# One dense batch instead of two in a block-sparse attention with a gated FFN: keys and queries of the block batches turned by TensorE, their V rows fetched through three queues

## The chip, the cores and the metric

The kernel runs on 1 core of one Trainium2 chip. The metric is the device time of one execution in microseconds (us); the median of three runs stands for a kernel. Everything said about the inside of an execution comes from one execution that the hardware profiler recorded.

## The reference

```python
# q, k, v: [4, 8, 768, 64] float32; sampled_blocks: [24, 3]; block = 32 positions, 24 blocks
scores = q @ k.transpose(0, 1, 3, 2) / sqrt(64)
mask = |blk_i - blk_j| <= 1  or  blk_i in (0, 23)  or  blk_j in (0, 23)
for qb in range(24):
    for kb in sampled_blocks[qb]:
        mask[block qb, block kb] = True
attn = softmax(where(mask, scores, -1e9)) @ v          # per batch and head
x  = attn, heads side by side: [3072, 512]
xn = x / sqrt(mean(x*x) + 1e-6) * rms_g
g  = xn @ w_gate                                       # [512, 1536]
out = (g * sigmoid(g) * (xn @ w_val)) @ w_out          # [3072, 512]
```

A query block so needs the first and the last key block, its neighbours, and three sampled ones, except for query blocks 0 and 23, which need all 24. The sampled block numbers are the same for all batches and heads, and they are known only when the kernel runs.

## The kernel before

A batch has 768 positions, that is six tiles of 128. The work is cut into units (`UNITS`, line 59): one to three tiles of one batch, for which attention, normalisation, FFN and output are done. The FFN of a tile is the largest part of TensorE's work: 96 projection matmuls per tile-equivalent (`proj`, L728, gate and value) and 12 output matmuls (`yy`, L767).

There are two kinds of batch, and `NDB` (line 51) says how many are of the first kind.

- A *dense* batch (0 and 1 before) computes all 768 keys for every query, and the mask is carried by 24 extra contraction rows (`AUG`, 64 + 24 = 88 rows). `dk` (L322) makes scores, `dexp` (L343) the exponentials, `dav` (L357) the product with V, `dxo` (L370) divides by the row sum. Keys and queries are turned so that the head dimension lies on partitions: batch 0 by TensorE (`tpx`, L301), batch 1 by DMA transposes from SP (`turn`, L288).
- A *block* batch (2 and 3 before) computes only the key blocks that are needed. Keys and queries are loaded, cast to bf16 (`fill_k`, `fill_q`), and turned by DMA transposes from SP (`turn_k` L478, `turn_q` L504). V is cast, written to a scratch tensor in HBM (`store_v`, L508), and read back as 32-row blocks by block number: `pair_v` (L570, L572, L578) fetches the blocks whose numbers are fixed, `block_v` (L555) the three sampled ones of a query block, whose row numbers sit in registers (`table_regs`, L435). The sampled key blocks are copied inside SBUF by GpSimd (`kg_sampled`), the fixed ones by VectorE or ScalarE (`kg_fixed`); both appear under the lines of the helper `copy` (ACT L144, POOL L146, DVE L148). `qk` (L599) and `exp` (L605) make an ordinary tile's scores and exponentials, `qka` (L615) and `expa` (L623) those of tile `AT`, which holds query blocks 0 and 23. `av` (L648) multiplies by V, `xo` (L659) divides.

After attention, for each unit: sum of squares (`sq`, L672 or L675), its inverse root (`rsq`, GpSimd L684, L686), scaling (`xq`, L693), a transpose to `xn` (by TensorE, `tr` L704, for the first `NPET` = 6 units, by a DMA transpose from SP, `xt` L715, for the later ones), then gate projection, tanh (`th`, ScalarE L737), `uu` (VectorE L743), value projection, `hp` (VectorE L754), output matmuls, `yo` (L777 or L779), and the store `so` (SP, L789 and L795).

The order of all this is made when the kernel is built. Every step is an operation with a list of engines that may do it, an estimated cost, steps that it depends on, and buffers that it takes and gives back. A loop (from L1204) always takes the operation that can start first by those estimates, with priorities deciding near-ties, and emits it. Each engine's instructions so stand in one fixed order, and an instruction that has to wait for a semaphore holds all that stands behind it on its engine. This holds for the queues that issue DMAs too: SP, ScalarE and GpSimd each issue theirs in order. The loads follow a list written out by hand (`seq`). Two of them are gated: `gate_sync` (L258) makes SP wait until a piece of the weights has landed. The weights themselves are loaded and cast by DMAs that GpSimd issues (L248, L252).

The pools that matter here: `vg` (gathered V tiles, 3), `kg` (gathered keys, 2), `xn`, `xq`, `xo` (2 units each), `hp` (2), `raw` (landing buffers for the block batches, 3).

Of the kernel before, what the change touches and what calls it, by code (L numbers as in the profile page):

```python
# [16 lines left out]
def kernel(  # L17
# [19 lines left out]
    P = 128  # L37
# [13 lines left out]
    NSLOT, NAUG, NOPEN, NDB = 5, 2, 2, 2  # L51
    IXAT, RGAT = 36.0, 48.0
    NPT, NPA, NKG, NVG, NRAW = 4, 2, 2, 3, 3
# [4 lines left out]
    HD = NC * D // 2  # L58
    UNITS = [(0, 0, 1), (0, 1, 1), (0, 2, 1), (0, 3, 3)]
    UNITS += [(b, c, 3) for b in range(1, NDB) for c in (0, 3)]  # L60
    ND = len(UNITS)
    for b in range(NDB, B):
        UNITS += [(b, (5, 0, 1), 3), (b, (2, 3, 4), 3)]
    NU = len(UNITS)
    HG = [("h", 0 if u < 3 else u) for u in range(NU)]
    HO = [u if u < 3 else 0 for u in range(NU)]
# [9 lines left out]
    def bank16(n):  # L76
# [12 lines left out]
    VAC = const.tile([P, 2, H * NC, D + 2], BF16, name="VAC")  # L89
    VGC = const.tile([P, 6, VW], BF16, name="VGC")  # L90
# [6 lines left out]
    RAWD = list(A)  # L97
    RAWS = [RAWC[:, i * RB:(i + 1) * RB] for i in range(NRAW)]
    aug = [AUG[:, i] for i in range(NAUG)]
    va_ = [VAC[:, i] for i in range(2)]  # L100
    vfl = [t.rearrange("p m d -> p (m d)")[:, 0:6 * VW] for t in va_]
    VAUG = [t.rearrange("p (t c h d) -> p t c h d", t=NC // 2, c=2, h=H) for t in (vfl[0], PTC[:, 10240:10240 + 6 * VW])]
    rt_ = RAWC[:, NRAW * RB:].bitcast(BF16)
    VGB = [VGC, rt_[:, 0:6 * VW].rearrange("p (x w) -> p x w", w=VW),
           vfl[1].rearrange("p (x w) -> p x w", w=VW)]
    PD = [PTC[:, i * PDW:(i + 1) * PDW] for i in range(3)]
    PTB = [t.rearrange("p (h l x) -> p h l x", h=2, l=2) for t in [rt_[:, 6 * VW:6 * VW + 1024]] + [
        PTC[:, i * 1024:(i + 1) * 1024] for i in range(NPT - 1)]]
    PAB = [PTC[:, 3072 + i * 2048:3072 + (i + 1) * 2048].rearrange("p (l h x) -> p l h x", l=2, h=2) for i in range(NPA)]
    KTB = [t.rearrange("p (a s) -> p a s", a=NP) for t in (xs_[3], xs_[1])]  # L110
    QTB = [t.rearrange("p (a s) -> p a s", a=NP) for t in (xs_[4], PTC[:, 7168:7168 + NP * S])]
    KGB = [xs_[i].rearrange("p (x a s j c) -> p x a s j c", x=6, a=NP, s=4, j=16) for i in (0, 2)]
    KROW = AUG[:, 0].rearrange("p i e c x -> p (i e c x)").rearrange(
        "p (a c t x) -> p a c t x", a=NP, c=2, t=NC // 2)
    QROW = AUG[:, 1].rearrange("p i e c x -> p (i e c x)").rearrange("p (a n x) -> p a n x", a=NP, n=NC)
    kvv = [t.rearrange("b h (t p c) d -> b p (h t) (c d)", p=P, c=2) for t in (k, v)]
    qvv = q.rearrange("b h (n p) d -> b n p h d", p=P)
# [32 lines left out]
    zt = const.tile([P, VW], BF16, name="zt")  # L150
# [36 lines left out]
    nc.gpsimd.memset(zt[0:32, P:VW], 0.0)  # L187
# [9 lines left out]
    for t in va_:  # L197
        nc.vector.memset(t[:, :, D:D + 1], 1.0)
# [72 lines left out]
    def load(g, i):  # L271
        b, pr = divmod(g, NP)
        if i == 0:
            rawd[g] = RAWD[held["rawd", g][1]]
        nc.sync.dma_start(out=rawd[g][:, i], in_=(kv, qv, vv)[i][b, :, 2 * pr:2 * pr + 2, :])

    def fill(g, i, eng):
        copy(eng, aug[g % NAUG][:, i, :, :, 0:D],
             rawd[g][:, i].rearrange("p h (c d) -> p h c d", d=D))

    def pad_v(g, eng):
        b, pr = divmod(g, NP)
        src = rawd.pop(g) if b else A[g]
        copy(eng, va_[b][:, 2 * pr * NC:2 * (pr + 1) * NC, 0:D],
             src[:, 2].rearrange("p h (c d) -> p (h c) d", d=D))

    def turn(g):
        nc.sync.dma_start_transpose(  # L288
            out=X[g % NSLOT].rearrange("p i e (c t) -> p (i e c) t", t=P),
            in_=aug[g % NAUG].rearrange("p i e c r -> p (i e c r)"))  # L290

    def zero_pad(i):
        nc.vector.memset(aug[i][:, :, :, :, KQ:P], 0.0)
# [15 lines left out]
    held, rawd = {}, {}  # L309
# [38 lines left out]
    def dav(u, pr, bk):  # L348
        b, c0, nt = UNITS[u]
        pt, va = pts.pop((u, pr)), va_[b]  # L350
        o_ = PS[:, bk[0], 0:nt * 2 * (D + 1)].rearrange(
            "p (t e d) -> p t e d", t=nt, e=2)
        tiles["o", u, pr] = o_
        for t in range(nt):
            for e in range(2):
                for jt in range(NC):
                    nc.tensor.matmul(  # L357
                        out=o_[:, t, e, :], lhsT=pt[:, jt, e, t * P:(t + 1) * P],
                        rhs=va[:, (2 * pr + e) * NC + jt, 0:D + 1],
                        start=(jt == 0), stop=(jt == NC - 1))  # L360
# [14 lines left out]
    tab_, at_ = VGB[0].rearrange("p x w -> p (x w)"), [0]  # L375

    def small(n, dt, p=P):
# [7 lines left out]
    kti, vti = small(NS * 2, I32, 1), small(NS * NR, I32, 1)  # L385
    koff, voff = {}, {}

    REGS = {"POOL": [("k", 0, 16), ("k", 16, 32), ("k", 32, 2 * NS)], "SP": [("v", 0, 16), ("v", 16, 32), ("v", 32, 2 * NS)],
            "ACT": [("v", 2 * NS, 2 * NS + 11), ("v", 2 * NS + 11, 3 * NS)]}
    HALF = 1024  # L390

    def load_table():
        nc.sync.dma_start(
            out=stab.rearrange("p n r i -> p (n r i)"), in_=s64.rearrange("n x -> (n x)").unsqueeze(0))
        for b in range(NDB, B):
            for lo in (0, S + 32):
                nc.sync.dma_start(out=vrows[b][lo:lo + 32, :], in_=zt[0:32, :])

    def table(i, eng):
# [3 lines left out]
        elif i == 1:  # L403
            TC(out=sf, in_=stab[:, 1:NB - 1, :, 0])
            TS(out=d2, in0=sf, scalar1=16.0, scalar2=None, op0=ALU.mult)
            TC(out=kti[:, 0:NS], in_=d2[:, :, 0])
# [16 lines left out]
        else:  # L423
# [4 lines left out]
            TS(out=vti.rearrange("p (r n) -> p n r", r=NR), in0=d2, scalar1=32.0, scalar2=32.0, op0=ALU.mult, op1=ALU.add)  # L428
# [3 lines left out]
    def table_regs(eng, part):  # L432
        e = {"POOL": nc.gpsimd, "ACT": nc.scalar, "SP": nc.sync}[eng]
        w, lo, hi = REGS[eng][part]
        _, got_ = nc.values_load_multi_w_load_instructions(  # L435
            {"k": kti, "v": vti}[w][0:1, lo:hi], engines=[e.engine], min_val=0,
            max_val={"k": 16 * (NB - 1) * (HALF + 1), "v": 32 * (NB + 1)}[w], skip_runtime_bounds_check_because=WHY)
        for i_, x in enumerate(got_):
            r, n = divmod(lo + i_, NS)
            {"k": koff, "v": voff}[w][n * NR + r] = x  # L440

    def k_at(n, r):
        x = koff[n * NR + min(r, 1)]
        if r:
            x = x >> 10 if r == 2 else x & (HALF - 1)
        return nc.s_assert_within(x, 0, 16 * (NB - 1), skip_runtime_bounds_check_because=WHY)


    def load_kv(b, i, hf):
        key = ("kv"[i], b, hf)  # L450
        raws[key] = RAWS[held["raw", key][1]]
        nc.sync.dma_start(
            out=raws[key].rearrange("p (x y) -> p x y", y=2 * D),
            in_=kvv[i][b, :, 3 * HH * hf:3 * HH * (hf + 1), :])

    def load_q(b, n):
        key = ("q", b, n // 3)
        raws[key] = RAWS[held["raw", key][1]]
        nc.sync.dma_start(
            out=raws[key][:, n % 3 * DM:(n % 3 + 1) * DM].rearrange("p (h d) -> p h d", h=H), in_=qvv[b, n])  # L460

    def fill_k(b, hf, c, eng):
        src = raws["k", b, hf].rearrange("p (a e t c d) -> p a e t c d", a=NP // 2, e=2, t=NC // 2, c=2)
        dst = KROW[:, NP // 2 * hf:NP // 2 * (hf + 1)].rearrange("p a c t (e d) -> p a c t e d", e=2)
        copy(eng, dst[:, :, c].rearrange("p a t e d -> p a e t d"), src[:, :, :, :, c, :])

    def fill_v(b, hf, c, eng):
        src = raws["v", b, hf].rearrange("p (h t c d) -> p h t c d", h=HH, t=NC // 2, c=2)
        vaugs[b] = VAUG[held["va", b][1]]
        copy(eng, vaugs[b][:, :, c, HH * hf:HH * (hf + 1), 0:D].rearrange("p t h d -> p h t d"), src[:, :, :, c, :])  # L470

    def fill_q(b, i, eng):
        copy(eng, QROW[:, :, 3 * i:3 * i + 3, :].rearrange("p a n x -> p n a x"),
             raws["q", b, i].rearrange("p (n a x) -> p n a x", n=3, a=NP))

    def turn_k(b):
        KTs[b] = KTB[held["KT", b][1]]
        nc.sync.dma_start_transpose(  # L478
            out=KTs[b].rearrange("p a (n x) -> p (a n) x", x=P), in_=KROW.rearrange("p a c t x -> p (a c t x)"))

    def tpk(b, pr, bk):
        t_ = bank16(bk[0])[:, 0:S].rearrange("p (c t x) -> p c t x", c=2, x=P)
        tiles["tk", b, pr] = t_
        for c in range(2):
            for t in range(NC // 2):
                nc.tensor.transpose(out=t_[:, c, t, :], in_=KROW[:, pr, c, t, :], identity=ident)

    def evk(b, pr, eng):
        KTs[b] = KTB[held["KT", b][1]]
        copy(eng, KTs[b][:, pr, :], tiles.pop(("tk", b, pr)).rearrange("p c t x -> p (c t x)"))  # L490

    def tpq(b, n, bk):
        t_ = bank16(bk[0])[:, 0:NP * P].rearrange("p (a x) -> p a x", x=P)
        tiles["tq", b, n] = t_
        for pr in range(NP):
            nc.tensor.transpose(out=t_[:, pr, :], in_=QROW[:, pr, n, :], identity=ident)

    def evq(b, n, eng):
        QTs[b] = QTB[held["QT", b][1]]
        copy(eng, QTs[b][:, :, n * P:(n + 1) * P], tiles.pop(("tq", b, n)))  # L500

# [821 lines left out]
```

## Time and profile before

| what | value |
|---|---|
| median of 3 runs | 305.85 us (304.5 to 306.33) |
| profiled execution | 307.95 us; its span 306.2 us |
| TensorE matmuls | 284.4 us busy, 93% of the span, 3838 instructions |
| VectorE | 195.1 us, 64% |
| ScalarE | 175.2 us, 57% |
| GpSimd | 80.3 us, 26% |
| DMA | 48.50 MB moved, mean 158 GB/s; 48037 of 85204 packets under 512 B |
| granted TensorE clock, mean | 0.989 of full |

The span is the time from the first to the last instruction of the program in the profile; the profiled execution's own time is 1.75 us longer. Matmuls are pipelined: a busy time counts each matmul from its start to its end, so a mean of 300 ns for one does not mean that one starts every 300 ns. What one costs in a stream is read from runs in the chain of work that ended last, where a piece has a length and a count. In the list of waits, a row says which instruction sat idle before it started and what released it.

### The profile page before, as it was taken

Reading aid. Unit: us, or ns where it says so; the run is one execution under the profiler, and the core shown is the slowest. Engines: PE = TensorE matmul, PEld = TensorE weight load, DVE = VectorE, ACT = ScalarE, POOL = GpSimd, SP = SyncE. Lnnn points to the kernel's source line nnn. Section 1 sums busy time; section 2 is a strip of 40 time slices with the busy share of each in tenths; the row PEclk is TensorE's granted clock in tenths of the full one; section 3 lists DMA queues with packets and bytes.
Section 4 is the critical chain, followed back from the end, with each engine's and each line's share of the span. In section 5 each row is a group of like instructions: output and inputs, shape, how many; then the busy total and the mean of one; then the engine's idle time right before and its main releaser. Section 6 shows DMA issues by size and latency. Waiting matters only on the chain.

```text
span 306.2 us, 9818 instructions
## 1 busy us (share of the span) xinstructions
PE 284.4 (93%) x3838; PEld 183.4 (60%) x3838; DVE 195.1 (64%) x462; ACT 175.2 (57%) x290; POOL 80.3 (26%) x196
## 2 busy tenths in 40 slices
PE   8999989889999998999779699998699999999995
PEld 7899877666666664665445345564255655546543
DVE  6688896576756755877568435767177958807700
ACT  4899874468888785368554226877065424413322
POOL 4648100010024615119754200755041000100000
PEclk9999999999999999999999979999989999999999
DMA  7999999864799996783987973333754400060032
GB/s 218 364 242 157 203 268 323 182 229 80 119 267 266 182 308 161 159 239 87 263 196 187 195 157 97 90 84 89 166 127 135 92 36 2 0 156 0 1 98 109
DMA packets 85204, 48.50 MB, mean 158 GB/s; under 512 B 48037, under 2 KB 81318, under 8 KB 85158
## 3 DMA queue, kind: packets, MB, share of 16 engines
q1 hardware_dynamic: 76946, 41.63, 54.7%
q0 software_dynamic: 5792, 4.72, 10.1%
q10 hardware_dynamic: 2420, 1.53, 2.0%
q8 instruction: 30, 0.49, 0.6%
q14 instruction: 16, 0.13, 0.1%
HBM read 36.70 MB, written 8.02 MB: 146 GB/s over the span
## 4 chain that ended last, share of the span: by engine, by line
PE 67%; DMA 14%; DVE 8%; issue 5%; SPq 2%; ACT 2%; ACTq 1%; DVEq 0%
PE PS L728 33%; PE PS L767 15%; PE PS L322 7%; PE PS L357 4%; DMA RAWC<-in_v_dram 4%; PE PS L648 3%; DMA XC<-AUG 2%; DMA RAWC<-in_k_dram 2%; PE PS L301 2%; DMA VGC<-vrows 2%; DVE uu L743 2%; PE PS L599 2%; DMA xn<-xq 1%; DVE hp L754 1%; ACT th L737 1%
## 5 line engine op out<-in xcount | busy, mean ns | idle before, releaser
L737 ACT ACTIVATE th<-PS 128x384 bf16<-128x384 f32 x96 | 46.5, 492 | 81.9 <-PE PS L728 37.5
L743 DVE SCALAR_TENSOR_TENSOR uu<-th,PS 128x384 bf16<-128x384 bf16 x96 | 52.4, 551 | 49.4 <-ACT th L737 47.1
L728 PE MATMUL PS<-xn,wg 128*128 128x384 bf16 (+1 forms) x480 | 74.3, 294 | 7.3 <-DVE uu L743 4.2
L343 ACT ACTIVATE PTC<-PS 128x768 bf16<-128x768 f32 x92 | 70.4, 815 | 14.0 <-PE PS L322 13.8
L728 PE MATMUL PS<-xn,wv 128*128 128x384 bf16 (+1 forms) x480 | 77.9, 297 | 0.1
L767 PE MATMUL PS<-wo,hp 128*128 128x512 bf16 (+1 forms) x300 | 71.4, 376 | 4.1 <-DVE uu L743 4.1
L754 DVE TENSOR_TENSOR hp<-uu,PS 128x384 bf16<-128x384 bf16 x96 | 52.0, 551 | 16.8 <-PE PS L728 14.7
L728 PEld LDWEIGHTS <-wg 128*128 128x128 bf16 x480 | 40.7, 98 | 31.4 <-issue 9.0
L146 POOL COPY XC<-XC 128x128 bf16 x132 | 39.3, 371 | 62.6 <-PE PS L599 35.7
L728 PEld LDWEIGHTS <-wv 128*128 128x128 bf16 x480 | 40.5, 98 | 23.9 <-issue 1.9
L767 PEld LDWEIGHTS <-hp 128*128 128x128 bf16 x300 | 29.0, 99 | 32.4 <-issue 6.2
L322 PE MATMUL PS<-XC 88*128 88x128 bf16 (+1 forms) x288 | 42.6, 276 | 0.6 <-ACT PTC L343 0.6
L322 PEld LDWEIGHTS <-XC 88*128 88x128 bf16 x288 | 22.2, 100 | 7.8 <-issue 0.9
L357 PE MATMUL PS<-VAC,PTC 128*128 128x65 bf16 x552 | 21.1, 193 | 0.2 <-DVE XO L370 0.2
L357 PEld LDWEIGHTS <-PTC 128*128 128x128 bf16 x552 | 20.0, 97 | 2.0 <-issue 0.3
L777 ACT ACTIVATE yo<-PS 128x512 f32<-128x512 f32 (+1 forms) x16 | 9.1, 571 | 20.2 <-PE PS L767 20.1
L146 POOL CAST AUG<-RAWC 128x768 bf16<-128x768 f32 (+3 forms) x12 | 11.6, 973 | 30.1 <-DMA RAWC<-in_k_dram 25.7
L693 DVE SCALAR_TENSOR_TENSOR xq<-XO,rs,gB 128x512 bf16<-128x512 f32 x24 | 18.5, 792 | 0.2 <-POOL rs L686 0.2
L686 POOL TENSOR_TENSOR rs<-ms,nhalf 128x1 f32<-128x1 f32 (+1 forms) x6 | 4.3, 714 | 47.8 <-DVE ms L675 47.8
L605 ACT ACTIVATE PTC<-PS 128x1024 bf16<-128x1024 f32 x15 | 15.2, 1022 | 1.6 <-PE PS L599 1.1
L648 PEld LDWEIGHTS <-PTC 128*32 128x32 bf16 x736 | 8.1, 97 | 8.7 <-issue 7.4
L599 PEld LDWEIGHTS <-XC 64*128 64x128 bf16 x480 | 7.5, 93 | 6.9 <-issue 5.8
(112 smaller groups left out, 225.1 us busy)
## 6 DMA issues: line engine op xcount, KB each, us to landing
out_dram<-yo SPq DMA_DIRECT2D x21, 256.0 KB, 2.0
RAWC<-in_k_dram SPq DMA_DIRECT2D x4, 768.0 KB, 5.7
RAWC<-in_v_dram SPq DMA_DIRECT2D x4, 768.0 KB, 10.6
RAWC<-in_q_dram SPq DMA_DIRECT2D x12, 256.0 KB, 5.3
RAWC<-in_v_dram SPq DMA_DIRECT2D x7, 384.0 KB, 6.5
RAWC<-in_k_dram SPq DMA_DIRECT2D x6, 384.0 KB, 6.6
wg<-in_moe_w_gate_dram POOLq DMA_DIRECT2D x4, 384.0 KB, 6.9
wv<-in_moe_w_val_dram POOLq DMA_DIRECT2D x4, 384.0 KB, 7.9
```

The costliest lines, as they stand in the source:

```text
L146: nc.gpsimd.tensor_copy(out=out, in_=in_)
L322: nc.tensor.matmul(out=s_[:, e, j * w:(j + 1) * w], lhsT=x[0:KQ, 0, e, jt * P:(jt + 1) * P], rhs=x[0:KQ, 1, e, c0 * P:c0 * P + w], start=T ...
L343: nc.scalar.activation(out=pts[u, pr][:, g * kt:(g + 1) * kt].rearrange("p j e w -> p e j w"), in_=s_[:, :, 0:kt * w].rearrange("p e (j w) ...
L357: nc.tensor.matmul(out=o_[:, t, e, :], lhsT=pt[:, jt, e, t * P:(t + 1) * P], rhs=va[:, (2 * pr + e) * NC + jt, 0:D + 1], start=(jt == 0), ...
L605: nc.scalar.activation(out=t_.rearrange("p h l x -> p (h l x)"), in_=tiles.pop(("s", b, n, pp)).rearrange("p h l x -> p (h l x)"), func=AF ...
L648: nc.tensor.matmul(out=o_[32 * i:32 * i + 32, a, :], lhsT=l_, rhs=r_, start=i not in begun, stop=k_ == last[i], tile_position=(0, 32 * i), ...
L693: nc.vector.scalar_tensor_tensor(out=xqs[u][:, t, :], in0=xos[u, t].rearrange("p h d -> p (h d)"), scalar=mss[u][:, t:t + 1], in1=gB, op0= ...
L728: nc.tensor.matmul(out=p_[:, j, :].rearrange("p (t w) -> p t w", w=P), lhsT=w_[:, c, f_ * P:(f_ + 1) * P], rhs=xns[u][:, :, c, :], start=( ...
L737: nc.scalar.activation(out=t_, in_=tiles["gp", u, f], func=AF.Tanh, scale=0.5)
L743: nc.vector.scalar_tensor_tensor(out=t_, in0=tiles.pop(("th", u, f)), scalar=1.0, in1=tiles.pop(("gp", u, f)), op0=ALU.add, op1=ALU.mult)
L754: nc.vector.tensor_tensor(out=hps[u][:, f * fg:(f + 1) * fg, :], in0=tiles.pop(("uu", u, f)), in1=tiles.pop(("vp", u, f)), op=ALU.mult)
L767: nc.tensor.matmul(out=tiles["yp", u, t, h], lhsT=hps[u][:, f, t * P:(t + 1) * P], rhs=wo[:, f, x], start=(f == 0), stop=(f == NF - 1))
```

## The change

- Batches 1, 2 and 3 are block batches now, batch 0 alone is dense (`NDB` = 1). Dense batch 1 disappears with its loads, its four DMA transposes and its V layout.
- A block batch's units are smaller: batch 1 has units of 1, 2, 1 and 2 tiles, batch 2 of 1, 2 and 3, batch 3 of 3 and 3. There are 13 units instead of 10; the first six are still those whose `xn` is turned by TensorE.
- Keys, queries and values of a block batch are loaded in two halves of four heads each, partition p taking positions 6p to 6p+5, which makes a contiguous run of 6 x 64 float32, 1536 bytes. Before, the runs were of 512 bytes (k, v) and 256 bytes (q).
- They are turned by 12 TensorE transposes per half (`turn`), copied from PSUM by ScalarE (`turned`) into position order. The scratch rows of V follow the same order (`store_v`).
- In tile `AT`, the first score matmuls take every sixth column of the turned keys as weights.
- The sampled V blocks of a query block (r = 0, 1, 2) are issued by SP, ScalarE and GpSimd; before, by SP (r = 0, 1) and ScalarE (r = 2). Two row numbers share a register, so ScalarE and SP load one set of 11 each; GpSimd's row number rides in its key register.
- Buffers: `vg` 4 instead of 3, `pt` 5 (shared by the `AT` tiles). A wait for the first value halves on a piece of the weights stands where it stood for dense batch 1.

The core of the diff, in the order of the file:

```diff
-    NSLOT, NAUG, NOPEN, NDB = 5, 2, 2, 2
+    NSLOT, NAUG, NOPEN, NDB = 5, 2, 2, 1
-    NPT, NPA, NKG, NVG, NRAW = 4, 2, 2, 3, 3
+    NPT, NKG, NVG, NRAW = 5, 2, 4, 3
+    SPLIT = (((5,), (0,1), (2,),( 3, 4)), ((5,), (0, 1), (2, 3, 4)), ((5, 0, 1), (2, 3, 4)))
     UNITS = [(0, 0, 1), (0, 1, 1), (0, 2, 1), (0, 3, 3)]
-    UNITS += [(b, c, 3) for b in range(1, NDB) for c in (0, 3)]
...
-        UNITS += [(b, (5, 0, 1), 3), (b, (2, 3, 4), 3)]
+        UNITS += [(b, ns, len(ns)) for ns in SPLIT[b - NDB]]
...
-    kvv = [t.rearrange("b h (t p c) d -> b p (h t) (c d)", p=P, c=2) for t in (k, v)]
-    qvv = q.rearrange("b h (n p) d -> b n p h d", p=P)
+    kvv = [kv, vv, qv]
...
+    REGS = {"POOL": [("k", 0, 16), ("k", 16, 32), ("k", 32, 2 * NS)],
+            "DVE": [...], "ACT": [("v", 0, NS // 2)],
+            "SP": [("w", 0, NS // 2)]}
...
+            TT(out=kti[:, 0:NS], in0=d1[:, :, 2], in1=k0f, op=ALU.add)
+            for t_, r in ((vti, 1), (wti, 0)):
+                TT(out=t_, in0=d1[:, NS // 2:NS, r], in1=d2[:, 0:NS // 2, r], op=ALU.add)
...
+            out=raws[key].rearrange("p (h y) -> p h y", h=HH), in_=kvv[i][b, :, HH * hf:HH * (hf + 1), :])
...
-    def turn_k(b):
-        nc.sync.dma_start_transpose(...)
...
+    def turn(b, x, j, bk):
+        t_ = PS[:, bk[0]:bk[0] + 2].rearrange("p b x -> p b x").bitcast(BF16)[:, :, 0:S].rearrange(
+            "p a (c w) -> p a c w", w=P)
+        tiles["turn", b, x, j] = t_
+        for a in range(2):
+            for c in range(NC):
+                nc.tensor.transpose(out=t_[:, a, c, :], in_=(KROW if x == "k" else QROW)[:, 2 * j + a, c, :], identity=ident)
+
+    def turned(b, x, j, eng):
+        ts, tb, n_ = (KTs, KTB, "KT") if x == "k" else (QTs, QTB, "QT")
+        ts[b] = tb[held[n_, b][1]]
+        copy(eng, ts[b][:, 2 * j:2 * j + 2, :].rearrange("p a (w c) -> p a c w", c=NC), tiles.pop(("turn", b, x, j)))
...
     def store_v(b):
         nc.sync.dma_start(
-            out=vrows[b][32:S + 32, :].rearrange("(t p c) f -> p t (c f)", p=P, c=2),
+            out=vrows[b][32:S + 32, :].rearrange("(p t) f -> p (t f)", t=NC),
...
-            copy(eng, kg[:, x, :, :, r, :], kt[:, :, :, bass.ds(kb, 16)])
+            copy(eng, kg[:, x, :, r, :], KTs[b][:, :, bass.ds(k_at(blocks(n)[x] - 1, r, eng), 32)])
...
-        (nc.scalar if r == 2 else nc.sync).dma_start(
+        (nc.sync, nc.scalar, nc.gpsimd)[r].dma_start(
...
-                    lhsT=KTs[b][HS[h], pr, m * P:(m + 1) * P] if m < NC else ...
+                    lhsT=KTs[b][HS[h], pr, m::NC] if m < NC else ...
...
+    CE = {1: (DP_, DP_, DP_), 2: (P_,D_,D_), 3: (DP_,DP_,P_)}      # engines of the casts of v, k, q
+    TTE, TTP = ("ACT",), -1
+    KDE, CPE = ("POOL", ), ("DVE", "ACT")
...
+        for x in "kq":
+            for j in range(2):
+                op(("tt" + x, b, j), {"PE": 12 * 0.056}, [("sf" + x, b, j, c) for c in range(2)], (TTP, b, j),
+                   lambda e, p, a=(b, x, j): turn(*a, p), [(S_, ("tt" + x, b, j))], [(x + "row", b)])
+                op(("turn" + x, b, j), pick_({"ACT": 1.45, "DVE": 1.75}, TTE), [("tt" + x, b, j)], (-0.5, b, j),
+                   lambda e, p, a=(b, x, j): turned(*a, e), [(x.upper() + "T", b)], [(None, ("tt" + x, b, j))])
...
+                for x in xs[::2]:
+                    op(("gv",) + G + (x,), {"SP": 2 * GVC}, sts + rgs["SP", "w"], (GVP, order, x),
+                       lambda e, p, a=G, x=x: [block_v(*a, x_, 0) for x_ in (x, x + 1)], [("vg", T)], d=0.2)
+                for x in xs:
+                    for r, e_, c_, w_ in ((1, "ACT", GVC, "v"), (2, "POOL", GPC, "k")):
+                        op(("gw",) + G + (x, r), {e_: c_}, sts + rgs[e_, w_], (GWP, order, x),
+                           lambda e, p, a=G + (x, r): block_v(*a), [("vg", T)])
```

## The prediction

> **What bounds the kernel now.** I read the page's slices first, then busy time by stage, the list of waits and the chain that ended last.
>
> ```profile
> PE   8999989889999998999779699998699999999995
> PEclk9999999999999999999999979999989999999999
> DMA  7999999864799996783987973333754400060032
> ```
>
> TensorE is 90% busy or more in most slices. It falls off in the sparse stage (slices 20 to 29), where PEclk dips twice.
>
> ```profile
> 62.00:120.00 58.00, 57.09 (x588) 37.50 (x587) 39.26 (x82) 46.31 (x69) 13.87 (x22) 1.00 0.94 207
> 120.00:250.00 130.00, 116.33 (x1962) 66.26 (x1961) 82.40 (x182) 67.09 (x118) 46.57 (x135) 0.97 0.58 142
> ```
>
> Columns: stretch, its length, busy us of PE, PEld, DVE, ACT, POOL, granted clock, DMA share, GB/s. Dense batch 1 (62 to 120) leaves PE 0.9 us idle. The two block batches (120 to 250) leave 13.7 us, and the clock costs 3.3 more: ten-us stretches show 0.84 at 170 and 0.83 at 220. That is 17.0 us that PE does not stream, 8.5 per block batch.
>
> ```profile
> PE PS L728 <- DVE uu L743: 4.2, 6, 1.2
> PE PS L767 <- DVE uu L743: 4.1, 2, 3.0
> PE PS L728 <- DMA xn<-xq: 3.1, 1, 3.1
> ACT th L737 <- DMA VAC<-vrows: 13.4, 2, 10.6
> ACT th L737 <- DMA VGC<-vrows: 6.0, 2, 3.5
> ACT th L737 <- DMA XC<-AUG: 5.8, 1, 5.8
> ```
>
> Columns: total us, times, longest. PE waits for `uu`, which waits for ScalarE's tanh, which stands in ScalarE's queue behind work that waits for a DMA. Two places in the chain (start, length, what) name those DMAs:
>
> ```profile
> 167.34 6.75 DMA XC<-AUG
> 175.04 0.50 ACT th L737
> ...
> 215.88 4.16 DMA xn<-xq
> ```
>
> So it is a PE-bound kernel with a leak in the block batches.
>
> **The change, part by part.** The profiled execution took 307.95 us, span 306.2; the median is 305.85. I work out a difference against the 306.2 and apply it to the median. Spacings of PE come from runs in the chain:
>
> ```profile
> 32.13 0.67 PE PS L728 x12
> ...
> 70.03 0.75 PE PS L704 x12
> ...
> 71.43 1.14 PE PS L357 x36
> 72.57 0.65 PE PS L322 x4
> ...
> 154.17 0.68 PE PS L599 x44
> ...
> 195.54 0.61 PE PS L615 x36
> ...
> 205.88 0.83 PE PS L648 x64
> ```
>
> *PE stream.* Dense batch 1 goes: 96 score matmuls at 0.1625 (0.65/4) are 15.6 us, 288 of P·V at 0.0317 are 9.1: -24.7. Its block form comes: 240 at 0.0155, 72 at 0.017, 448 at 0.013: +10.7. Turning K and Q on PE: 144 transposes at 0.0625 (the L704 row, the same kind of instruction): +9.0. Transposes of xn fall from 48 to 36: -0.75. Narrower units: a one-tile unit's projections cost 96 x 0.0558 = 5.36 us a tile against 96 x 0.1625/3 = 5.20. Three more such units are +0.5; six tiles in two-tile units have no row, lie between 0 and +1.0, and I take 0.5. Sum: **-4.8**. The 144 score matmuls whose weights are now read with a step of six elements have no row either: 0 if the load stays under the matmul, at most +5.9 by the slowest weight load (L301, 138 ns mean against 97); I take 0, since weight loads of 93 to 100 ns sit under matmuls 16 ns apart in L599.
>
> The Trainium skill (TensorE: Matmul & The Clock Gate, Part 4: PE-mode transpose) speaks against this: about 275 ns per transpose in one kernel, and the full clock does not engage for transposes. Here L704 takes 219 ns each, but twelve pass in 0.75 us at clock 1.00. By the page's figure as a spacing, the 144 would be 39.6 us and the kernel slower; the trace decides.
>
> *The K and Q transposes by DMA go.* There were eight, which held SP's queue for 3.6 to 6.4 us each. The one at 167.34 shows on PE as 3.03 us idle (busy 6.97 of 170 to 180) plus 1.6 of clock: **-4.6**. The other end is 0, if the PSUM copy on ScalarE that takes its place comes as late.
>
> *V rows from three queues.* SP issues 22 single blocks per block batch instead of 44, beside some 17 pair and edge pieces: 39 in place of 61, a third less. From 140 to 160 PE is 4.2 us short (9.03 and 6.74 busy), waiting for gathered rows and for work behind them. I take half: **-2.1** (0 to -4.2). At 211 to 215.9 SP was issuing V rows while the finished `xq` (last DVE piece ends 210.7) waited for its transpose behind them; 210 to 220 is short 4.06 us, plus 1.7 of clock. Half again: **-2.9** (0 to -5.8). Against it: seven units, not four, now take that DMA transpose.
>
> *What it adds on ScalarE, VectorE, GpSimd and DMA*, costed at nothing under PE's FFN work. ScalarE loses 48 exponentials (39 us at 0.815) and gains 14 of 1.02, 12 PSUM copies of 1.44 (the 128x1536 copy to xn took 1.44), some 20 copies of 0.48 and 22 issues of 0.32: about +9 on 175, less 7 for output copies that pass to VectorE. If the cover goes, the tanh is late next, then `uu`, then PE. VectorE gains about 9 on 195 (12 normalisations at 0.60 and 12 output copies at 0.68, minus 8 normalisations at 0.75). DMA moves some 5 MB more of V rows in a stretch at share 0.58. The loads in 1536-byte runs get no credit: the dense batches' 384 KB in such runs landed in 6.5 us, 768 KB in short runs in 5.7 and 10.6.
>
> GpSimd needs its own budget, per block batch:
>
> ```profile
> L146 POOL COPY XC<-XC 128x128 bf16 x132 | 39.3, 371 | 62.6 <-PE PS L599 35.7 <-PE PS L322 10.5 <-DMA XC<-AUG 8.3
> L248 POOL DMA_DIRECT2D wg<-in_moe_w_gate_dram x4 | 3.5, 887 | 0.0
> L248 POOL DMA_DIRECT2D wv<-in_moe_w_val_dram x4 | 3.1, 786 | 0.0
> ```
>
> 66 sampled copies at 0.371 are 24.5; 22 new issues at 0.85 (the weight loads, the only issues from this queue; the lower end is ScalarE's 0.32, the upper the first one's 1.15) are 18.7; casts 5, rsqrt 4: 52 us. PE needs about 61 for the same batch (six tiles at 5.2 + 2.6 of FFN, 10.7 attention, 3 transposes). It fits, with 9 us to spare.
>
> The Trainium skill (SBUF — State Buffer, SBUF: two separate sides) speaks against GpSimd as issuer: while VectorE runs a copy in a two-port mode GpSimd cannot write descriptors, and 620 ns became 3100. The eight weight issues above took 0.74 to 1.15 us in stretches with VectorE 80% busy. By the page's 3.1 the 22 issues are 68 us and GpSimd bounds the kernel, some 40 us per batch slower; by the row, nothing.
>
> *Register loads.* ScalarE loads its row numbers once instead of twice (4.1 and 5.4 us at 50 and 57). PE is 1.7 us short from 50 to 70: **-0.9**.
>
> *A third block batch.* Of the 17.0 us, 17.0 - 4.6 - 2.1 - 2.9 = 7.4 stay for two batches, so the third brings **+3.7** (1.2 if only what I could not place recurs, 8.5 if nothing is mended).
>
> *Hand-over from dense to block.* Before, batch 1 was dense and covered all preparation of batch 2. Now batch 1 is fetched behind the weights (gates at 32.3 and 36.3, unchanged). V's second half, issued 36.9, lands by 47.5 (10.6); casts behind register loads (3.6 each on GpSimd) end near 53; the store, K's second half and Q follow on SP's queue and land near 65; six V issues on GpSimd (5.1) stand before Q's cast; transpose and PSUM copy (0.75 + 1.44) make the first score possible near 73. PE had its last dense P·V at 59.6 and in the new order some 25 groups of 0.67 before that score: near 75. The margin of 2 is smaller than the spread of one landing (5.7 to 10.6). I take one wait as long as the two of 3.0 and 3.1 seen: **+3.0** (0 to 5).
>
> Sum: -4.8 - 4.6 - 2.1 - 2.9 + 3.7 - 0.9 + 3.0 = -8.6, so 305.85 - 8.6 = **297.3 us**, the span near 297.6.
>
> **Rivals.**
> *ScalarE's queue decides (slower).* 66 V-row issues stand in it in place of 44, each waiting for a buffer or for the store, with tanh behind them. Then block batches cost what they cost now, 17.0/44 = 0.39 us per issue, so 22 more are +8.5; the ScalarE copy stands in the same queue, so the 4.6 is not saved; nothing is halved: -4.8 + 8.5 - 0.9 + 3.0 = +5.8, 311.7 us. It decides once such a wait exceeds the two groups (1.3 us) that PE has in hand. For it: the 21 us of tanh waiting for V rows. Against: a fourth V buffer.
> *Block batches run without leaks (faster).* All bounds at their good end: -4.8 - 4.6 - 4.2 - 5.8 + 1.2 - 1.7 + 0 = -19.9, 286 us. For it: units of one and two tiles give PE other units' FFN in each chain; SP's queue loses 33 us of transposes. Against: ScalarE, VectorE and GpSimd would all be near 80% there, in fixed order.
> *GpSimd bounds.* From 1.25 us per issue it passes PE's 61; at 2.0 that is 16.5 per batch, 347 us. Against: the highest row is 1.15.
> *The PE saving alone, leaks as large as before plus a third batch's 3.7 and the hand-over:* about 307, no change.
>
> **How the numbers follow.** Main case 0.40, leak-free 0.20, ScalarE 0.24, GpSimd 0.04, no change 0.12. A measurement of this kernel tells about 1% (3 us) from no change. Faster by over 1%: nearly all of the main case and the leak-free one, 0.58; within 1%: 0.14; slower: 0.28. The main case's own range is 291 to 303; leaving out two in ten, 287 to 313.
>
> **What would show it.** Right: transposes on PE 12 in about 0.75 us; no PE wait behind a K transpose; PE short by about 11 us over the three block batches; GpSimd's V issues near 0.85 us and GpSimd under PE; a wait of about 3 us between 60 and 76. Wrong: tanh waiting over 30 us in all for V rows (ScalarE's case), GpSimd issues over 1.25 us, or block-batch idle as large per batch as now.

## The result, and the profile after

The changed kernel takes **337.22 us** (median of 4 runs, 334.84 to 341.73); the kernel before took 305.96 beside it. The ratio is 1.1006, 95% interval 1.0902 to 1.111: 10% slower, where 297.3 us was forecast. The profiled execution took 335.35 us; its span is 333.8. A run more than 1.5% above the fastest of its kernel is left out of every ratio, so a ratio need not be that of the two medians.

The page's slices of the changed kernel (rows: TensorE, ScalarE, granted clock):

```profile
PE   8997899587779967969578869999999999999995
ACT  5998376178986899795967599557717422422310
PEclk9999599878979997879879999999999999999999
```

TensorE has holes from 58 to 200 us (a slice is 8.3 us), the clock falls in or just behind the same places (and at 33 to 42, behind a smaller hole), and ScalarE is at 8 or 9 in most of them. Busy time by stage, first of the changed kernel, then of the kernel before (columns: stretch, its length, busy us of PE, PEld, DVE, ACT, POOL, then clock, DMA share, GB/s):

```profile
20.00:80.00 60.00, 50.41 (x701) 41.84 (x703) 36.89 (x108) 37.83 (x47) 17.14 (x26) 0.89 0.84 190
80.00:230.00 150.00, 124.34 (x2475) 89.65 (x2490) 80.61 (x179) 120.19 (x135) 83.14 (x231) 0.92 0.55 157
```

```profile
20.00:80.00 60.00, 56.97 (x836) 45.05 (x834) 44.83 (x126) 44.41 (x69) 8.27 (x13) 1.00 0.95 202
80.00:230.00 150.00, 136.55 (x2099) 80.67 (x2095) 93.44 (x203) 89.82 (x148) 58.46 (x153) 0.98 0.75 172
```

Length less busy time times clock is what TensorE does not stream. Before it is 3.0 us in the first stretch and 16.2 in the second; after, 60 - 50.41 x 0.89 = 15.1 and 150 - 124.34 x 0.92 = 35.6. That is 31.5 us more, while the span grew by 27.6: by this difference TensorE's own work shrank by some 4 us, and waits ate it several times over. The clock is part of the loss: of the 35.6 us, 25.7 are idle time and 9.9 are lost to the lower clock.

In the list of waits (us in total, times, longest), V rows in front of tanh are a small item now (in the changed kernel L702 is tanh, L708 `uu`, L468 the new transposes, L580 the first scores of tile `AT`, L148 a ScalarE copy):

```profile
DVE uu L708 <- ACT th L702: 65.6, 42, 8.3
PE PS L580 <- ACT XC L148: 5.4, 2, 3.1
PE PS L468 <- ACT XC L148: 4.8, 2, 2.7
ACT th L702 <- DMA VXC<-vrows: 4.5, 1, 4.5
```

Tanh waited 19.4 us for V rows in the two largest rows before; now 4.5 and 3.2. Yet `uu` waits for tanh 65.6 us, up from 47.1, and TensorE waits for ScalarE's copies. The groups of instructions, shapes apart (count | busy us, mean ns | idle before), show why:

```profile
L148 ACT COPY XC<-PS 128x1536 bf16<-128x1536 bf16 x8 | 42.3, 5292 | 9.1 <-PE PS L468 9.1
L148 ACT COPY VXC<-PS 128x1536 bf16<-128x1536 bf16 x4 | 21.2, 5298 | 5.3 <-PE PS L468 5.3
```

The twelve copies of turned keys and queries (`turned`, through `copy`) take 5.29 us each. The forecast had 1.44. Together they are 63.5 us instead of 17.3. ScalarE's timeline shows what such a copy does:

```profile
139.37 5.31 ACT L148 COPY XC<-PS 128x1536 bf16<-128x1536 bf16 x1 [0.68 <-PE PS L468]
144.29 0.81 ACT L702 ACTIVATE th<-PS 128x512 bf16<-128x512 f32 x1
144.99 5.29 ACT L148 COPY XC<-PS 128x1536 bf16<-128x1536 bf16 x1
```

```profile
145.87 1.28 PE L693 MATMUL PS<-xn,wg 128*128 128x256 bf16 x8 [2.83 <-DVE uu L708]
```

One tanh comes through between two copies. TensorE (second fence, its timeline) stands for 2.83 us until `uu` behind that tanh frees its bank.

### The profile page after: what moved, and what is told of

It reads as the page before. It is cut to its first block, busy times and chain, and to the rows that moved or that the text cites. A ratio compares the mean times of both kernels' runs of the same rounds, so it can differ in the third digit from the quotient of the medians.

```text
span 333.8 us, 11910 instructions
## 1 busy us (share of the span) xinstructions
PE 292.1 (88%) x4605; PEld 206.4 (62%) x4634; DVE 198.3 (59%) x470; ACT 210.3 (63%) x269; POOL 131.5 (39%) x343
## 4 chain that ended last, share of the span: by engine, by line
PE 62%; ACT 13%; issue 9%; DMA 7%; DVE 3%; ACTq 2%; SPq 1%; POOLq 1%; POOL 1%; DVEq 0%
PE PS L693 33%; PE PS L732 14%; ACT XC L148 7%; PE PS L613 4%; DMA wg<-in_moe_w_gate_dram 4%; ACT VXC L148 4%; PE PS L564 3%; PE PS L305 3%; ACTq L520 2%; DMA VXC<-vrows 2%; PE PS L340 2%; ACT th L702 2%; DMA RAWC<-in_k_dram 1%; PE PS L580 1%; DVE uu L708 1%
## 5 line engine op out<-in xcount | busy, mean ns | idle before, releaser
L708 DVE SCALAR_TENSOR_TENSOR uu<-th,PS 128x384 bf16<-128x384 bf16 (+1 forms) x90 | 51.9, 579 | 67.6 <-ACT th L702 65.6
L702 ACT ACTIVATE th<-PS 128x384 bf16<-128x384 f32 (+1 forms) x90 | 47.7, 534 | 66.3 <-PE PS L693 51.5
L693 PE MATMUL PS<-xn,wg 128*128 128x128 bf16 (+2 forms) x624 | 79.5, 277 | 10.1 <-DVE uu L708 6.5
L693 PE MATMUL PS<-xn,wv 128*128 128x128 bf16 (+2 forms) x624 | 78.7, 272 | 0.3 <-DVE hp L719 0.3
L719 DVE TENSOR_TENSOR hp<-uu,PS 128x384 bf16<-128x384 bf16 (+1 forms) x90 | 51.0, 578 | 19.7 <-PE PS L693 17.4
L148 ACT COPY XC<-PS 128x1536 bf16<-128x1536 bf16 (+1 forms) x9 | 42.7, 4745 | 9.8 <-PE PS L468 9.1
L326 ACT ACTIVATE PTC<-PS 128x768 bf16<-128x768 f32 x44 | 32.9, 815 | 6.8 <-PE PS L305 6.8
L148 ACT COPY VXC<-PS 128x1536 bf16<-128x1536 bf16 x4 | 21.2, 5298 | 5.3 <-PE PS L468 5.3
L148 ACT COPY XC<-XC 128x256 bf16<-128x256 bf16 (+1 forms) x44 | 17.9, 451 | 8.5 <-PE PS L564 7.2
L305 PE MATMUL PS<-XC 88*128 88x128 bf16 (+1 forms) x192 | 22.1, 251 | 0.6 <-ACT PTC L326 0.4
L564 PEld LDWEIGHTS <-XC 64*128 64x128 bf16 x720 | 11.6, 94 | 12.4 <-issue 10.2
L520 POOL DMA_DIRECT2D VXC<-vrows x36 | 18.3, 510 | 2.5 <-issue 0.9
L468 PE MATMUL PS<-ident,AUG 128*128 128x128 bf16 x144 | 11.0, 229 | 8.9 <-ACT XC L148 4.8
L468 PEld LDWEIGHTS <-AUG 128*128 128x128 bf16 x144 | 9.5, 102 | 10.6 <-issue 5.4
```

The source lines that it names most:

```text
L148: nc.scalar.copy(out=out, in_=in_)
L305: nc.tensor.matmul(out=s_[:, e, j * w:(j + 1) * w], lhsT=x[0:KQ, 0, e, jt * P:(jt + 1) * P], rhs=x[0:KQ, 1, e, c0 * P:c0 * P + w], start=T ...
L326: nc.scalar.activation(out=pts[u, pr][:, g * kt:(g + 1) * kt].rearrange("p j e w -> p e j w"), in_=s_[:, :, 0:kt * w].rearrange("p e (j w) ...
L520: (nc.sync, nc.scalar, nc.gpsimd)[r].dma_start(out=new_vg(g, n)[32 * r:32 * r + 32, x, :], in_=vrows[g][bass.ds(v_at(blocks(n)[x] - 1, r), ...
L564: nc.tensor.matmul(out=s_[:, h, pl, lo:lo + 32 * m], lhsT=kg[HS[h], x, pr], rhs=q_of(b, n, i, m, HS[h], pr), start=True, stop=True)
L693: nc.tensor.matmul(out=p_[:, j, :].rearrange("p (t w) -> p t w", w=P), lhsT=w_[:, c, f_ * P:(f_ + 1) * P], rhs=xns[u][:, :, c, :], start=( ...
```

## The experiments

Two theories stood against each other. **A**: the copies hold tanh, and TensorE waits. **B**: the loss is elsewhere, in the hand-over from dense to block work, the third block batch, or the narrow units.

Code below is shortened; `t_` is the tile in PSUM that a copy reads.

**e1_contig: the same copies, written without a step.** In the changed kernel a copy's output goes to every sixth element, because position is `6 w + c` and each transpose delivers one `c`. Here the elements are written one behind the other, which leaves out the position order.

```
-  copy(eng, ts[b][:, 2*j:2*j+2, :].rearrange("p a (w c) -> p a c w", c=NC), t_)
+  copy(eng, ts[b][:, 2*j:2*j+2, :].rearrange("p a (c w) -> p a c w", w=P), t_)
```

> The changed kernel with one edit: the twelve ScalarE copies of turned keys and queries (L148, out of PSUM, 128x1536) write their outputs one element behind the other instead of with a step of 6 elements. The position order of the keys and queries is left out by this, so the block batches' outputs are not the reference's; every instruction and its order stay. Theory A (the copies with a step take 5.3 us where 1.44 was costed; 12 of them are 46 us more on ScalarE, tanh stands behind them, and TensorE waits for tanh): the copies fall to 1.4 to 1.6 us, ScalarE's busy time from 210 to about 164 us, and the time from 337 to 298 to 310. Rival B (the loss is in the hand-over to the block batches, the third block batch itself, the narrow units and the clock that falls with them): the copies may fall too, but the time stays above 325. In between (310 to 325): both.

Measured: copies 1.44 us each, ScalarE 166.4 us busy, median 309.21 us. Its nine runs lie between 304.2 and 311.9 us; the ratio to the kernel before, 0.9894 (0.984 to 0.9947), is over three of them. Theory A holds; B had said above 325, and no run came near that.

**e2_stepread: the step moved to the read.** The same elements go to the same places, with the loops turned round.

```
+  copy(eng, ts[b][:, 2*j:2*j+2, :].rearrange("p a (w c) -> p a w c", c=NC),
+       t_.rearrange("p a c w -> p a w c"))
```

> The changed kernel with the loops of the twelve copies turned round: same elements to the same places, but now written one behind the other, and read from PSUM with a step of 128 elements (256 bytes). If the price lies in writing with a step (A1), the copies take 1.4 to 1.6 us and the time is 298 to 310 as with the contiguous copies; if a step on either side costs the same (A2), they stay near 5.3 us and the time near 337; if the price comes from runs of one element whatever side, between 3 and 5.3, with a time of 315 to 337. Rival B: above 325 in every case.

Its groups (columns as above):

```profile
L148 ACT COPY XC<-PS 128x1536 bf16<-128x1536 bf16 x8 | 11.5, 1439 | 13.7 <-PE PS L468 7.6 <-DMA RAWC<-in_v_dram 3.5 <-DMA VXC<-vrows 2.5
```

1.44 us: reading PSUM with a step of 256 bytes costs nothing here; writing SBUF with a step of 12 bytes costs 3.85 us per copy. The time is 308.69 us, ratio 1.0061 (1.0019 to 1.0104). So 28.5 of the 31.3 us lost against the kernel before were this one loop order (by the two ratios, 28.9). Whether e1_contig is a little faster than this is open: by the ratios it is, by the medians it isn't, and its runs are spread over 7.7 us.

**e3_dve and e4_both: the copies on VectorE, or on both engines.**

```
-  TTE, TTP = ("ACT",), -1
+  TTE, TTP = ("DVE",), -1          # e4_both: ("ACT", "DVE")
```

> The changed kernel with the twelve copies (same step of 6 elements in the write) on VectorE instead of ScalarE, and the schedule that the planner makes of it at its own cost of 1.75 us. Theory A: ScalarE loses 63.6 us of work, tanh isn't held any more; if VectorE writes with a step at its usual pace (384 elements from PSUM took 0.551 us, so 1536 some 1.2 to 2.2), the time is 297 to 312; if VectorE pays the same 5.3 us, its 198 us become 262, the hold goes over to uu and hp behind the copies, and the time stays at 325 to 345. Rival B: above 325 though the copies are short and off ScalarE.

> The changed kernel with the twelve copies shared between ScalarE and VectorE as the planner deals them at its costs of 1.45 and 1.75 us. Theory A: the time lies between that of copies on ScalarE alone (337) and on VectorE alone, in proportion to the copies that are still on ScalarE (each some 2.5 to 3.3 us of the end). Rival B: no more than 6 us from 337.

```profile
L152 DVE COPY XC<-PS 128x1536 bf16<-128x1536 bf16 x8 | 42.4, 5294 | 5.3 <-PE PS L468 5.2
```

VectorE pays the same price (e3_dve's groups; its contiguous copy of this size takes 0.96). The times are 349.35 us (ratio 1.1406, 1.1321 to 1.1491) and 349.06 (1.1357, 1.1292 to 1.1422). The hold moves to `uu` and `hp`, as A said for that case, though 4 us past its range. For e4_both A missed: seven of the twelve copies went to VectorE, and the time should have lain between 337 and 349. Why it lies at 349 was not looked into. Both kernels were planned anew at costs of 1.45 and 1.75 us, so orders differ too.

**l1_steps: other steps.** Keys' copies write with a step of 2 elements, queries' with 3; everything else as in the changed kernel.

```
+  n2 = 2 if x == "k" else 3
+  copy(eng, ts[b][:, 2*j:2*j+2, :].rearrange("p a (y w c) -> p a y c w", c=n2, w=P), t_ rearranged by "p a (y c) w -> p a y c w")
```

> The changed kernel (twelve copies on ScalarE, written with a step) with other steps in the write: keys' six copies with a step of 2 elements, queries' six with a step of 3, instead of 6 (the position order is left out by this; the instructions and their order stay). Theory A1 (any write of single 2-byte elements with gaps pays, whatever the gap): all near 5.3 us, time 330 to 340. Theory A3 (the price grows with the step): keys' copies 1.3 to 2.7 us, queries' 2 to 4 us, time 308 to 325.

ScalarE's timeline, one copy of each kind:

```profile
65.73 1.89 ACT L148 COPY XC<-PS 128x1536 bf16<-128x1536 bf16 x1 [5.59 <-PE PS L468]
78.15 2.73 ACT L148 COPY VXC<-PS 128x1536 bf16<-128x1536 bf16 x1
```

1.44, 1.89, 2.73 and 5.29 us at steps of 1, 2, 3 and 6. From 2 to 3 that is 0.84 us per step, from 3 to 6 0.85: the price grows with the step, 0.55 ns per element and step (0.85 us over 1536). The one run took 305.6 us, under A3's range. Its copies are 10.5 us longer in all than e2_stepread's (27.7 against 17.2), and it is no slower. As far as one run shows, then, copies of up to 2.7 us hide, and only those of 5.3 cost time: the loss is not in proportion to the copies' length.

**h1_vgate, h2_table, h3_wide: what is left, by the planner.** At 308.7 us the forecast is still 11 us away. In e2_stepread the first stretch still loses 60 - 51.28 x 0.91 = 13.3 us, while the second loses only 150 - 139.77 x 0.99 = 11.6, less than before the change:

```profile
20.00:80.00 60.00, 51.28 (x724) 42.30 (x726) 39.15 (x112) 34.71 (x53) 20.24 (x34) 0.91 0.86 191
80.00:230.00 150.00, 139.77 (x2987) 101.37 (x3005) 100.19 (x214) 95.22 (x155) 99.09 (x281) 0.99 0.67 179
```

So the hand-over is the place. Two causes show there. Theory C: SP issues the block batch's two V loads (1.5 MB) at 19.5 us, among the weights. "The change" above says that the wait for the weights stands in front of the value halves; that is not so. The code gates the key halves (`i == 0` of `"kvq"`), and the list of loads now begins with V. SP's timeline in e2_stepread (`scr<-wv` is a gate):

```profile
19.47 0.95 SPq L447 DMA_DIRECT2D RAWC<-in_v_dram  x2
37.00 0.72 SPq L261 DMA_DIRECT2D scr<-wv  x1
37.84 0.37 SPq L447 DMA_DIRECT2D RAWC<-in_k_dram  x1
```

A piece of `wg` lands 11.4 us after its issue, against 6.9 in the kernel before (the issues of e2_stepread, then of the kernel before; the last number is the median time to landing):

```profile
wg<-in_moe_w_gate_dram POOLq DMA_DIRECT2D x4, 384.0 KB, 11.4
```

```profile
wg<-in_moe_w_gate_dram POOLq DMA_DIRECT2D x4, 384.0 KB, 6.9
```

TensorE stands 2.05 us for `wg` from 27 and 1.92 us for `wo` from 46. Theory D: at 62 it waits for a cast that stands behind register loads on GpSimd (timelines of e2_stepread, GpSimd and TensorE):

```profile
65.02 1.60 POOL L150 CAST AUG<-RAWC 128x768 bf16<-128x768 f32 x2 [4.50 <-issue]
```

```profile
65.90 0.82 PE L468 MATMUL PS<-ident,AUG 128*128 128x128 bf16 x6 [3.63 <-POOL AUG L150]
```

Each was first mended through the planner, and the narrow units were undone:

```
h1_vgate  -  gate = 2 + hf if b == NDB and i == 0 else None        # K
          +  gate = 2 + hf if b == NDB and i == 1 else None        # V
h2_table  -  IXAT, RGAT = 36.0, 48.0
          +  IXAT, RGAT = 24.0, 34.0
h3_wide   +  SPLIT = (((5, 0, 1), (2, 3, 4)),) * 3
```

> The kernel with the copies read with a step and written contiguously (308.7 us), and one more edit: the first block batch's two V loads (1.5 MB, issued at 19.5 us among the weights) wait for the weights' third and fourth quarter as K's did. Theory C (the loads crowd the weights: wg lands 11.4 us after its issue against 6.9 in the kernel before, and TensorE waits 2.2 us at 27 and 2.1 us at 46): wg's landing falls under 9 us, both waits go, and the time falls by 2 to 5 us, to 303.5 to 306.5. Rival D (what is short is the hand-over at 60 us, where a GpSimd copy stands 4.5 us behind register loads): the waits for weights go but the later V rows lengthen the hand-over, time 307 to 312.

> The kernel with the copies read with a step (308.7 us), and the table of sampled blocks worked out, and its registers loaded, from 24 and 34 us of the planner's time instead of 36 and 48, where GpSimd is idle (36.5 to 55 us). Theory D (register loads ahead of GpSimd's copies hold the first turning by 3.6 us at 62, and the clock dips after it): the wait at 62 falls under 1 us and the time by 3 to 6 us, to 302.5 to 306. Theory C: no more than 1.5 us.

> The kernel with the copies read with a step (308.7 us), with every block batch in two units of three tiles, as the third one has, instead of units of 1, 2, 1, 2 and 1, 2, 3 tiles: fewer and wider matmuls (480 rather than 624 of L693). If narrow units only cost their 1.0 us of TensorE time: 306 to 309. If they give overlap (units end earlier, so there is FFN work to put between the steps of attention), wide ones lose it: 312 to 322. If they hold something up: 300 to 306.

Measured: h1_vgate 310.78 us (ratio 1.0162, 0.9993 to 1.0332); h2_table 320.02 (1.0447, 1.0274 to 1.062); h3_wide 310.88 (1.0161, 1.0032 to 1.029). The first two removed the wait they aimed at: `wg` landed after 8.4 us in h1_vgate, and the wait at 62 is gone in h2_table. Both gave it back in the block stage: the stretch from 20 to 80 lost 7.3 and 11.0 us (13.3 in e2_stepread), the one from 80 to 230 lost 20.6 and 26.7 (11.6). The planner, told of the changed times, makes a new order for every engine, which is the likely reason: h1_vgate lost 4.7 us of TensorE between 100 and 120 (15.28 busy), h2_table had new waits of TensorE, 2.5 to 3.2 us each, at 58, 107, 132, 171 and 176. They decide nothing on theories C and D. h3_wide can't be told from e2_stepread: the intervals overlap.

**j1_reglate, j2_vgate, j3_both: the same two edits with every engine's order kept.** The planner is not told; only the emission changes.

```
j1_reglate  +  if o["key"] == ("gw", NDB, AT, 2, 1): late()          # ahead of the first V row
            +  if o["key"] == ("rg", "POOL", 2): late = <its emission>
            +  elif o["fn"] is not None: ...
j2_vgate    -  if gate:
            +  if gate or a[:2] == (NDB, 1): gate_sync(2 + a[2])
```

> The kernel with the copies read with a step (308.7 us), every engine's order kept but for one thing: GpSimd's third group of register loads (4.5 us, ahead of its two casts of keys at 65.0 us) is issued behind its casts for the first block batch and ahead of the first V rows. Theory D (the register loads hold the first turning of keys: TensorE waits 3.6 us at 62, and the clock dips to 0.73 there): the wait falls under 1 us, the clock between 60 and 70 stays above 0.9, the time falls by 3 to 5.5 us to 303 to 306. Rival E (the wait moves on: V rows that GpSimd issues come later, tanh behind ScalarE's, or the next key load sets the time): less than 1.5 us, 307 to 309.

> The kernel with the copies read with a step (308.7 us), every engine's order kept, with two more tiny transfers on the sync engine's queue, which make the first block batch's two V loads wait for the weights' third and fourth quarter. Theory C (those 1.5 MB crowd the weights): wg lands 7 to 9 us after its issue instead of 11.4, the waits of 2.2 us at 27 and 2.1 us at 46 go, the time falls by 2.5 to 5 us to 303.5 to 306. Rival E: V and K loads of the batch move behind each other, the hand-over at 60 us takes back what is won: 307.5 to 311.

> Both of these edits. If they are independent: 298 to 303, which is where the forecast for the change lay (297.3). If the one takes the other's gain: 304 to 308.

Measured: j1_reglate 305.43 us (ratio 0.9925, 0.9889 to 0.9962), with TensorE busy from 60 to 70 and the clock at 1.00 there; j2_vgate 303.42 (0.9867, 0.9815 to 0.9919), with `wg` landing after 7.8 us and both waits for weights gone; j3_both **300.64** (0.9738, 0.9675 to 0.9801). Against e2_stepread's median that is 3.3, 5.3 and 8.1 us. The kernel before, run beside each, gives 4.2, 6.0 and 9.9 us by the ratios. Either way the two add up, C and D both hold, and j3_both is faster than the kernel before too, by 2.6%. Its first stretch loses 60 - 55.92 = 4.1 us:

```profile
20.00:80.00 60.00, 55.92 (x827) 43.90 (x823) 46.72 (x125) 41.33 (x62) 27.68 (x56) 1.00 0.95 217
```

**k1_twoq: the third queue taken away.** On e2_stepread, SP issues the third sample's V rows again.

```
-  (nc.sync, nc.scalar, nc.gpsimd)[r].dma_start(
+  (nc.sync, nc.scalar, nc.sync)[r].dma_start(           # and SP loads 22 more registers
```

> The kernel with the copies read with a step (308.7 us), with the 66 V-row transfers of the third sampled block issued by the sync engine again (22 register loads more there) instead of GpSimd, at the same places of the plan: the part 'V rows from three queues' half undone. If that part is worth what the forecast gave it (5.0 us): 312 to 316. If V rows are not what ends waits here: 307.5 to 310. If GpSimd's issues of 0.51 us cost more than they bring: 304 to 307.

Measured: 337.45 us (ratio 1.098, 1.0927 to 1.1034), 29 us more, far past every expectation. SP's timeline in k1_twoq, then in e2_stepread:

```profile
90.91 11.11 SPq L526 DMA_DIRECT2D PTC<-vrows  x15
```

```profile
88.74 6.33 SPq L520 DMA_DIRECT2D PTC<-vrows  x8
```

The next batch's V load stands behind these issues and goes out at 102.1 instead of 95.2 us; its second K load at 112.3 instead of 106.0. Tanh waits 20.7 us for the `PTC` V rows (5.4 in e2_stepread). The 22 register loads on SP are not what costs: they take 4.5 us at 52.7, and the stretch from 20 to 80 loses 11.1 us (13.3 in e2_stepread). The loss is in the block stage, 150 - 123.17 x 0.91 = 37.9 us against 11.6:

```profile
80.00:230.00 150.00, 123.17 (x2544) 88.41 (x2543) 80.94 (x176) 81.34 (x129) 57.10 (x176) 0.91 0.57 157
```

The planner still counted these issues on GpSimd, so part of the 29 us may belong to an order that doesn't fit; that was not separated.

## Why the prediction was wrong, point by point

- **The step that failed** is the sentence that costed the added work "at nothing under PE's FFN work" with "12 PSUM copies of 1.44 (the 128x1536 copy to xn took 1.44)". The row was of the same shape, but of a contiguous write; the new copies write every sixth element. The diff shows that step, and the forecast did weigh a step for matmul weights, but not for the copy's output. Measured: 5.29 us each, 46.2 us more on ScalarE in bursts of 5 us, 28.5 us of time. What the cover could not take was the length of one copy, more than the sum of them (as far as l1_steps' one run shows). The chain behind it was named ("tanh is late next, then `uu`, then PE"), and that is the chain seen.
- The Trainium skill (SBUF — State Buffer, Door 1: The DMA port swizzle) says that SBUF has lines of 16 bytes, that at least two accesses per line are needed for full bandwidth, and that 8 bf16 elements are so how far one can step for free. The runs differ: writes with steps of 2 and 3 elements (4 and 6 bytes, at least two per line) already take 1.89 and 2.73 us against 1.44.
- **Hand-over, +3.0 (0 to 5).** The wait came where it was forecast (60 to 76), for a cast behind register loads: 4.1 us in the changed kernel, 3.6 in e2_stepread. But the stretch from 20 to 80 lost 13.3 us in e2_stepread against 3.0 before, 10 more. The forecast took the gates as "unchanged" and V's second half as issued at 36.9; the V loads had slipped out from behind the gates and went out at 19 us (5.3 us of time by j2_vgate). It also let the register loads end by 53, where GpSimd ran them until 65 (3.3 us by j1_reglate).
- **K and Q transposes, -4.6, and V rows, -2.1 and -2.9, with +3.7 for the third batch**: together -5.9 in the block stage. With the copies mended that stage lost 11.6 us instead of 16.2: -4.6. In the changed kernel itself the other end named for the first of them ("0, if the PSUM copy ... comes as late") came true, and more. How the gain divides among them was not measured, but in k1_twoq the third queue's going costs 29 us, far more than the forecast's 5, with an order that was planned for three queues.
- **PE stream, -4.8.** Taking the lost time of the two stretches off the span's difference leaves -3.9 (27.6 - 31.5) for the changed kernel, -4.7 (1.0 - 5.7) for e2_stepread and -2.7 (-8.6 + 5.9) for j3_both. About right. The transposes passed as forecast, twelve in 0.68 us at a granted clock of 1.00 (five such rows in the changed kernel's chain), and the 1.0 for narrow units is too small to see in h3_wide.
- **GpSimd** was costed too high, on the safe side. Its groups in the changed kernel:

```profile
L150 POOL COPY XC<-XC 128x128 bf16 x198 | 53.4, 316 | 66.8 <-PE PS L564 32.9 <-PE PS L580 24.0 <-ACT XC L148 9.2
L520 POOL DMA_DIRECT2D VXC<-vrows x36 | 18.3, 510 | 2.5 <-issue 0.9 <-PE PS L693 0.2
```

  Issues took 0.51 us, not 0.85, and copies 0.316, not 0.371. The rival in which GpSimd bounds falls.
- **The rival in which ScalarE's queue decides** had the engine right and the cause wrong: tanh waited 7.7 us for V rows in the changed kernel and 13.2 in e2_stepread, not over 30. It was the length of a copy, not an issue waiting for a buffer.
- Of the signs named, "no PE wait behind a K transpose" and "short by about 11 us" failed (10.2 us in the two rows above alone; 35.6 us), and "block-batch idle as large per batch as now" came true as the sign of being wrong (35.6 us over three batches, 11.9 each, against 8.5). With the copies and the hand-over mended the time is 300.6 us, 3.3 above the forecast and in its main range of 291 to 303. That it comes so close is partly luck: the forecast's -8.6 was -4.8 of stream and -3.8 of waits, j3_both's span is also 8.6 shorter than before, but by -2.7 and -5.9.

## What to carry to other kernels

Price a copy by its whole access pattern, not by its shape: when a row of the old trace is taken as the cost of a new instruction, compare step and destination first, and put a permutation on the side that reads PSUM. When the source of a load list changes, check which load its gates now stand in front of. And test an edit with all orders kept: a gate in front of the same V loads was worth 5 us that way and nothing when a planner was allowed to answer it.

## What the runs showed of the hardware that was not expected

- ScalarE and VectorE, 128x1536 bf16 from PSUM to SBUF: written with a step of 6 elements both take 5.29 us, where contiguous copies take 1.44 and 0.96. Two engines of different pace meet at one price, so the limit appears to be on the writing side; that was inferred, not measured by itself.
- By three points, the price is linear in the step from 2 on (1.89, 2.73, 5.29 us at 2, 3, 6), while ScalarE's read of PSUM with a step of 256 bytes is free (1.44 us).
- A GpSimd issue of a 32.5 KB V-row transfer takes 0.51 us, less than its issues of weight loads of 384 and 768 KB (0.76 to 0.89).
